# Float64 weights made float32 with the sign and upper exponent on ScalarE and one joining instruction on VectorE, and 34 evictions moved from ScalarE to VectorE

## The chip, the cores and the metric

The kernel runs on one core of one Trainium2 chip. The metric is the device time of one execution in microseconds. Before the change the median of three runs is 370.74 us (370.56 to 374.9). The engines are called PE (TensorE, matrix products), ACT (ScalarE), DVE (VectorE), POOL (GpSimd) and SP (SyncE, which issues the DMA transfers).

## The reference

```python
attn = softmax(mask(q @ k.T / 8)) @ v            # 2 batches x 12 heads, 448 tokens, 64 wide, causal
x = attn as (896 tokens, 768)
x = soft mixture of 8 experts x 4 slots:          # dispatch and combine weights from softmax of x @ phi
    slots = dispatch.T @ x; slot_out = relu(slots @ w1) @ w2; x = combine @ slot_out
out = ((x @ w_a) * (x @ w_b)) @ w_out             # w_a, w_b 768 x 1536, w_out 1536 x 768
```

q, k, v, phi, w1, w2 are float32. The weights w_a, w_b and w_out are drawn and scaled in double precision and come as **float64**: 8 bytes each, 28.3 MB of the 90 MB that the kernel reads. The chip computes in float32, so these 3.5 million numbers have to be turned into float32 inside the kernel.

A float64 has 1 sign bit, 11 exponent bits and 52 mantissa bits. In memory byte 7 (the last) holds the sign and the upper 7 exponent bits, byte 6 the lower 4 exponent bits and the top 4 mantissa bits, and bytes 5, 4 and 3 the next mantissa bits. A float32 of the same number needs the sign, 8 exponent bits with another offset, and the top 23 mantissa bits.

## The kernel before

**Attention stage** (to about 135 us). Heads are taken two at a time, 12 iterations `it`, each in four steps `g` = 0 to 3, in a software pipeline written out by hand (the instruction order of every engine is the order of the code). A step of iteration `it` does: scores of one group of query blocks on PE (`scores`, tile `s`, three PSUM buffers) with the row maxima on DVE (tensor_reduce, tile `nm`); in step 0 also the product with V of iteration it-2 (`pv`, tile `v`, evicted by ACT to `xT`); four transposes of the probabilities of iteration it-1 (`transp`, tile `t` in PSUM, two buffers), whose result is evicted to one quarter of `pT`; the exponentials of the step's scores on ACT (`softmax`, tile `p`); sums and reciprocals on DVE (`norm`, tile `rc`) and the scaling of `p` by them on POOL (line 294). Once per iteration `xtr` turns `xT` back by four transposes (tile `xt`) and evicts them to `x_sb`. The order in which the four quarters of `pT` are turned is `TORD = (1, 3, 0, 2)`. Of them ACT evicts quarters 1, 0 and 2 (line 314); quarter 3 (`TDVE = 1` is its position) is evicted by DVE in `evict`, line 318. ACT also evicts `x_sb`, line 360.

**Conversion.** Between these steps `conv_step` converts one "raw" tile (128 partitions x 768 doubles, 768 KB) at a time; `CVN = (1, 1, 0, 1)` gives three per iteration, after steps 0, 2 and 3. 32 of the 36 raw tiles are converted in the attention stage, the last four (halves of w_out) among the expert products. A raw tile is loaded by SP into one of four ring slots (`NR = 4`), and the slot is free for the next load when DVE has done its part (`used`). Per tile ACT makes two passes (`widen`): line 164 scales the upper word of each double, read as a float32, into the destination, line 165 turns the lower word into an integer in place. One conversion later (`LAG = 1`) DVE joins them in two instructions: line 195 puts the sign bit beside the low bits, line 198 shifts the destination left by three and ORs the low bits in. `widen` and `conv_step` can also put the two passes on POOL, for steps after `LASTQ`; no conversion of the profiled execution does so.

**Expert and output stages** (from about 135 us). The experts' weights w1, w2 stream through the ring (64 tiles of 768 KB), while the combined products of w_a, w_b and w_out are formed beside them.

Of the kernel before, what the change touches and what calls it, by code (L numbers as in the profile page):

```python
# [33 lines left out]
NT1 = 32  # L34
WPRE = (0, 10, 13, 17)
TORD = (1, 3, 0, 2)
SCQ = 1
TDVE = 1
TILES = (
    (("rect", 4, 4, 0, 4), ("rect", 8, 4, 0, 8), ("rect", 12, 4, 0, 12), ("tri", 0, 4), ("sq", 0, 8)),  # L40
    (("rect", 16, 4, 0, 16), ("rect", 20, 4, 0, 13), ("tri", 4, 2)),
# [19 lines left out]
CEND = 1  # L61
# [19 lines left out]
LASTQ = (11, 3)  # L81
# [9 lines left out]
def moe_kernel(ctx: ExitStack, tc: tile.TileContext, pk, vt, phi, w1, w2, wab, wo, rsel, out):  # L91
    nc = tc.nc

    const = ctx.enter_context(tc.tile_pool(name="const", bufs=1))
# [39 lines left out]
    x_sb = {}  # L134
# [11 lines left out]
    raw = {}  # L146

    def load_raw(i, slot):
        t = slot_tile(slot, I32, f"raw{i}")
        nc.sync.dma_start(out=t, in_=(wab[i // 2] if i < 24 else wo[i // 2 - 12])[:, 768 * (i % 2):768 * (i % 2) + 768].bitcast(I32))  # L150
        raw[i] = t

    def widen(t, dst, lo, n, low):
        pr = t.rearrange("p (c w) -> p c w", w=2)[:, lo:lo + n, :]
        hi, lw = pr[:, :, 1].bitcast(F32), pr[:, :, 0].bitcast(U32)
        if low == "pool":
            nc.gpsimd.tensor_scalar(
                out=dst, in0=hi, scalar1=2.0 ** -112, scalar2=1.0, op0=ALU.mult, op1=ALU.mult
            )
            nc.gpsimd.tensor_scalar(  # L160
                out=pr[:, :, 0], in0=lw, scalar1=2.0 ** -29, scalar2=-0.49999, op0=ALU.mult, op1=ALU.add
            )
        else:
            nc.scalar.activation(out=dst, in_=hi, func=AF.Copy, scale=2.0 ** -112)  # L164
            nc.scalar.activation(out=pr[:, :, 0], in_=lw, func=AF.Copy, scale=2.0 ** -29, bias=-0.49999)  # L165
        return dst.bitcast(I32), pr[:, :, 0], pr[:, :, 1]

    conv = []
    fin = []
# [13 lines left out]

    queue_conv(0, 36)

    def conv_step(n, lag=LAG, limit=36, low="act"):
        for _ in range(n):
            if conv and conv[0] < limit:
                i = conv.pop(0)
                dst = conv_dst(i)  # L190
                done.append(i)
                fin.append((i,) + widen(raw[i], dst, 0, 768, low))
            while len(fin) > (lag if conv and conv[0] < limit else 0):
                i, di, b, ph = fin.pop(0)
                nc.vector.scalar_tensor_tensor(  # L195
                    out=b, in0=ph, scalar=-0x80000000, in1=b, op0=ALU.bitwise_and, op1=ALU.bitwise_or
                )
                nc.vector.scalar_tensor_tensor(  # L198
                    out=di, in0=di, scalar=3, in1=b, op0=ALU.logical_shift_left, op1=ALU.bitwise_or
                )  # L200
                used("raw", i)

# [7 lines left out]
    for i in range(2):  # L210
        t = ap.tile([128, PCOLS], F32, name=f"p{i}", bufs=1)
# [87 lines left out]
    def transp(it, b):  # L299
        d = st[it]  # L300
        if b == TORD[0]:
            d["pT"] = ap.tile([128, 16, 128], F32, tag="pT", bufs=1, name=f"pT{it}")
        ps = psT.tile([128, 4, 128], F32, tag="t", name=f"t{it}_{b}")
        for j in range(4):
            kt, i = TBLK[4 * b + j]
            o = POFF[i] + 128 * kt
            nc.tensor.transpose(ps[:, j, :], d["p"][:, o:o + 128], ident)  # L307
        dst = d["pT"][:, 4 * b:4 * b + 4, :]
        if it == 11 and b in (TORD[1], TORD[3]):
            nc.vector.tensor_copy(out=dst, in_=ps)  # L310
        elif it < 11 and b == TORD[TDVE]:
            d["pt"] = dst, ps
        else:
            nc.scalar.activation(out=dst, in_=ps, func=AF.Copy)  # L314

# [189 lines left out]
    with tc.manual_schedule():  # L505
# [15 lines left out]
        for it in range(13):  # L521
            if 1 <= it < 12:
                load_v(it)
            for g in range(4):
                if it == 1:
                    warmup(NW2)
                if it < 12:
                    scores(it, g)
                if g == 0 and it >= 2:
                    pv(it - 2)  # L530
                if it >= 1:
                    transp(it - 1, TORD[g])
                if it < 12:
                    softmax(it, g)
                if g:
                    if it < 12:
                        norm(it, BANKS[g - 1] if it == 11 else ((), BANKS[0] + BANKS[1], BANKS[2])[g - 1])
                elif it:
                    norm(it - 1, BANKS[3])
                if g == SCQ and it + 1 < 12:  # L540
                    begin(it + 1)
                if g == 3 and it + 2 < 12:
                    load_qk(it + 2)
                if (it, g) in DSP:
                    dispatch0(DSP.index((it, g)))
                if it >= 2 and g == (3 if it == 8 else 1):
                    xtr(it - 2)
                if it in (4, 7, 10) and g == 2:
                    logits((it - 4) // 6, (0, 1, 2) if it != 7 else (3, 4, 5))
                step += 1  # L550
                if step > CVOFF:
                    conv_step(CVN[step % len(CVN)], LAG, NT1, "pool" if (it, g) > LASTQ else "act")
                if g == TDVE and 1 <= it < 12:
                    evict(it - 1)
        pv(11)
        xtr(11)
# [688 lines left out]
def layout(inp):  # L1245
    import numpy as np

    q, k, v = inp["q"], inp["k"], inp["v"]
    c = np.ascontiguousarray

    def tr(t):
        return t.reshape(12, 2, S, 64).transpose(0, 1, 3, 2).reshape(12, 128, S)

    v12 = v.reshape(12, 2, S, 64)
    vm = v12[:, :, :384].reshape(12, 2, 3, 128, 64).transpose(0, 3, 2, 1, 4).reshape(12, 128, 384)
    wa, wb, wo = inp["moe2_w_a"], inp["moe2_w_b"], inp["moe2_w_out"]
    rs = np.zeros((64, 5, 2, 128), np.float32)
# [41 lines left out]
```

## Time and profile before

| | |
|---|---|
| median of three runs | 370.74 us |
| span of the profiled execution, first to last instruction | 370.0 us |
| busy in the span: PE, DVE, ACT, POOL | 90%, 62%, 55%, 25% |
| from 20 to 130 us: PE, DVE, ACT, POOL | 99.6, 104.6, 108.2, 71.7 us of 110 |
| mean granted clock of TensorE | 0.985 |

The profiled execution's span is 0.7 us under the median; what lies around the span is not shown. The page's shares are means over stages that differ: in the attention stage ACT and DVE are busy nearly all the time, from 150 to 200 us the DMA queues are, and in the last 70 us PE is. A table by stretches is therefore read before any share of the whole.

### The profile page before, as it was taken

To read this page: it belongs to the slowest core of one execution; us is meant where nothing else is said; L and a number is where in the kernel's file an instruction comes from. 1 tells how busy PE (TensorE), PEld (TensorE's weight loads), DVE (VectorE), ACT (ScalarE), POOL (GpSimd) and SP (SyncE) were. 2 spreads that over 40 slices of the span, in tenths; PEclk is the share of its full clock that TensorE was granted. 3 is DMA by queue.
4 is the path that set the end of the run, shared out by engine and by line. 5 is a ranking of instruction groups with operands and counts; after the bars stand their busy time and mean duration, and the time that the engine had idled before them with its cause. 6 is when DMAs were issued, how large, how long until landed. Compare 5 with 4: busy or idle time off the path is not lost.

```text
span 370.0 us, 6891 instructions
## 1 busy us (share of the span) xinstructions
PE 334.6 (90%) x2551; PEld 201.8 (55%) x2551; DVE 230.1 (62%) x620; ACT 202.0 (55%) x464; POOL 91.1 (25%) x128
## 2 busy tenths in 40 slices
PE   8897898989989978988988889999899889999996
PEld 5454454544544655343342346634565359899995
DVE  3689989999999962021025887507856669933121
ACT  2599999999999952103007445414546732422221
POOL 2457666667766510001000000000000110301110
PEclk9999989999999999999999989999999999999999
DMA  7677789998677787999999999778910000001222
GB/s 282 269 240 282 273 309 389 345 341 288 247 280 280 245 289 308 390 421 416 418 332 402 396 338 351 263 317 272 421 78 2 0 1 2 0 2 43 85 87 85
DMA packets 20224, 90.51 MB, mean 245 GB/s; under 512 B 2336, under 2 KB 5024, under 8 KB 20192
## 3 DMA queue, kind: packets, MB, share of 16 engines
q1 hardware_dynamic: 20192, 90.09, 65.2%
q8 instruction: 20, 0.33, 0.4%
q14 instruction: 12, 0.10, 0.1%
HBM read 87.33 MB, written 2.75 MB: 243 GB/s over the span
## 4 chain that ended last, share of the span: by engine, by line
PE 46%; ACT 27%; DVE 16%; issue 4%; DMA 3%; POOL 3%; ACTq 0%; POOLq 0%; DVEq 0%
ACT p L278 8%; PE o L1172 8%; PE M L891 8%; PE h L651 5%; PE so L692 4%; ACT raw L165 4%; PE ab L777 4%; ACT wab L164 4%; DVE pf L833 3%; ACT pT L314 3%; PE s L257 3%; DVE pt L832 3%; DMA raw<-in_wo_dram 3%; POOL p L294 3%; ACT wo L164 2%
## 5 line engine op out<-in xcount | busy, mean ns | idle before, releaser
L294 POOL TENSOR_SCALAR p<-p,rc 128x448 f32<-128x448 f32 (+6 forms) x84 | 69.2, 837 | 46.4 <-DVE rc L291 36.9
L257 PE MATMUL s<-qk 64*64 64x448 f32 (+6 forms) x336 | 48.5, 403 | 0.1
L1076 POOL TENSOR_TENSOR cc<-gt,cc 128x512 fp32r<-128x512 f32 (+1 forms) x6 | 6.9, 1156 | 157.6 <-ACT cc L1075 157.6
L278 ACT ACTIVATE p<-s,nm 128x448 f32<-128x448 f32 (+6 forms) x84 | 40.0, 492 | 7.8 <-DVE nm L268 7.6
L891 PE MATMUL M<-wt,P_t 128*128 128x384 f32 x168 | 35.9, 356 | 4.1 <-DVE P_t L864 1.3
L307 PE MATMUL t<-ident,p 128*128 128x128 f32 x192 | 33.7, 293 | 5.1 <-POOL p L294 5.1
L195 DVE SCALAR_TENSOR_TENSOR raw<-raw 128x768 int32<-128x768 int32 x36 | 35.2, 978 | 3.0 <-ACT raw L165 3.0
L263 DVE TENSOR_REDUCE nm<-s 128x1 f32<-128x448 f32 (+6 forms) x84 | 31.7, 411 | 8.0 <-PE s L257 8.0
L891 PEld LDWEIGHTS M<-wt,P_t 128*128 128x128 f32 x168 | 29.1, 193 | 13.6 <-ACT wt L885 4.8
L345 PE MATMUL v<-pT,v 128*64 128x448 f32 (+3 forms) x192 | 26.9, 396 | 7.9 <-ACT pT L314 7.7
L165 ACT ACTIVATE raw<-raw 128x768 int32<-128x768 uint32 x36 | 33.9, 941 | 0.0
L651 PE MATMUL h<-w,sT 128*32 128x512 f32 x192 | 29.9, 614 | 3.2 <-DMA w<-in_w_dram 2.3
L257 PEld LDWEIGHTS s<-qk 64*64 64x64 f32 x336 | 19.9, 136 | 21.3 <-issue 15.6
L307 PEld LDWEIGHTS t<-ident,p 128*128 128x128 f32 x192 | 20.7, 142 | 17.6 <-POOL p L294 7.3
L885 ACT ACTIVATE wt<-wo 128x384 fp32r<-128x384 f32 x48 | 21.8, 513 | 13.6 <-PE M L891 13.1
L886 DVE TENSOR_TENSOR wt<-wo,wt 128x384 fp32r<-128x384 f32 x48 | 23.8, 552 | 8.5 <-ACT wt L885 8.5
L198 DVE SCALAR_TENSOR_TENSOR wab<-wab,raw 128x768 int32<-128x768 int32 x24 | 27.9, 1162 | 0.8
L777 PE MATMUL ab<-wab,sT 128*32 128x384 f32 x288 | 27.5, 498 | 0.5 <-DVE sT L616 0.5
L692 PE MATMUL so<-w,hpad 128*32 128x384 f32 x256 | 24.8, 493 | 0.9 <-ACT wt L885 0.4
L314 ACT ACTIVATE pT<-t 128x512 f32<-128x512 f32 x35 | 21.7, 619 | 5.5 <-PE t L307 5.0
L345 PEld LDWEIGHTS v<-pT,v 128*64 128x64 f32 (+1 forms) x192 | 10.9, 134 | 22.6 <-ACT pT L314 14.0
L164 ACT ACTIVATE wab<-raw 128x768 f32<-128x768 f32 x24 | 23.1, 962 | 0.0
(155 smaller groups left out, 519.5 us busy)
## 6 DMA issues: line engine op xcount, KB each, us to landing
w<-in_w_dram SPq DMA_DIRECT2D x64, 768.0 KB, 8.0
raw<-in_wab_dram SPq DMA_DIRECT2D x24, 768.0 KB, 5.3
raw<-in_wo_dram SPq DMA_DIRECT2D x12, 768.0 KB, 4.4
qk<-in_pk_dram SPq DMA_DIRECT2D x12, 448.0 KB, 4.9
v<-in_pk_dram SPq DMA_DIRECT2D x12, 192.0 KB, 5.5
out_dram<-ost SPq DMA_DIRECT2D x6, 384.0 KB, 2.3
v<-in_vt_dram SPq DMA_DIRECT2D x12, 32.0 KB, 5.3
out_dram<-ost SPq DMA_DIRECT2D x2, 192.0 KB, 1.9
```

What stands on the lines that cost most here:

```text
L164: nc.scalar.activation(out=dst, in_=hi, func=AF.Copy, scale=2.0 ** -112)
L165: nc.scalar.activation(out=pr[:, :, 0], in_=lw, func=AF.Copy, scale=2.0 ** -29, bias=-0.49999)
L195: nc.vector.scalar_tensor_tensor(out=b, in0=ph, scalar=-0x80000000, in1=b, op0=ALU.bitwise_and, op1=ALU.bitwise_or)
L257: nc.tensor.matmul(sb[r, o:o + n], lhsT=qT[r, 64 * i:64 * i + 64], rhs=kT[r, 0:n], start=False, stop=True, skip_group_check=True,)
L278: nc.scalar.activation(out=d["p"][:, POFF[i]:POFF[i] + n], in_=sb[:, o:o + n], func=AF.Exp, bias=d["nm"][:, c:c + 1], scale=d["scale"], ac ...
L294: nc.gpsimd.tensor_scalar(out=p[:, POFF[i]:POFF[i] + n], in0=p[:, POFF[i]:POFF[i] + n], scalar1=rc[:, CIX[i]:CIX[i] + 1], scalar2=1.0, op0 ...
L307: nc.tensor.transpose(ps[:, j, :], d["p"][:, o:o + 128], ident)
L345: nc.tensor.matmul(ps[r, 128 * kt:S], lhsT=lhsT, rhs=rhs, start=(kt == 0), stop=(kt == 3), skip_group_check=True)
L651: nc.tensor.matmul(ps[32 * g:32 * g + 32, :], lhsT=sT[:, 0, c, :], rhs=wt[8 * e + i // 3][:, 512 * (i % 3):512 * (i % 3) + 512], start=(i ...
L692: nc.tensor.matmul(so[32 * g:32 * g + 32, 0:384], lhsT=t[:, c, :], rhs=wt[8 * e + 4 + i // 4][:, 384 * (i % 4):384 * (i % 4) + 384], start ...
L777: nc.tensor.matmul(abps[q][32 * g:32 * g + 32, 0:384], lhsT=sT[:, 1, c, :], rhs=w[:, c % 2, 384 * g:384 * g + 384], start=(c == 0), stop=( ...
L891: nc.tensor.matmul(mps[k][h][:, 0:384], lhsT=l[:, f, :], rhs=r, start=(n == 0 and i == 0), stop=(n == 11 and i == 2))
```

## The change

Each raw tile is read from 3 bytes further on, so that a tile's first 32-bit word of each pair holds bytes 3 to 6 of a double, and the byte after it holds byte 7. `wab` and `wo` become flat arrays with 1024 doubles of zeros behind them, so that the last row may run over. The transfer is written in bytes (6144 per partition instead of 1536 words), the bytes that move are as many.

ACT still makes two passes. The first reads byte 7 as a signed 8-bit integer, with the activation function Prelu (one slope for positive and another for negative arguments) and a bias of -56 read from a [128, 1] column `shr`. The second is applied to the first's result in place, again Prelu with a bias column, and writes an integer: the sign and the upper exponent bits in their float32 position. DVE then makes one instruction in place of two: the word of bytes 3 to 6 shifted right by five, ORed into the destination.

Two positions of `TORD` go from ACT to DVE for iterations 0 to 10 (`TDV2 = (2, 3)`, quarters 0 and 2: 22 evictions of 128x512), and all 12 evictions of `x_sb` (112x512). The choice of POOL for late conversions is dropped.

```diff
@@
-TDVE = 1
+TDVE = (1,)
+TDV2 = (2,3)
@@
+    shr = const.tile([128, 2], F32, name="shr")
+    nc.vector.memset(shr[:, 0:1], -56.0)
+    nc.vector.memset(shr[:, 1:2], 112.0 * 2.0 ** -13)
@@ load_raw
-        nc.sync.dma_start(out=t, in_=(wab[i // 2] if i < 24 else wo[i // 2 - 12])[:, 768 * (i % 2):768 * (i % 2) + 768].bitcast(I32))
+        src, n = (wab, i // 2) if i < 24 else (wo, i // 2 - 12)
+        at = (n * 128 * 1536 + 768 * (i % 2)) * 8 + 3
+        rows = src.bitcast(U8)[at:at + 128 * 12288].rearrange("(p b) -> p b", b=12288)
+        nc.sync.dma_start(out=t.bitcast(U8), in_=rows[:, 0:6144])
@@ widen
-            nc.scalar.activation(out=dst, in_=hi, func=AF.Copy, scale=2.0 ** -112)
-            nc.scalar.activation(out=pr[:, :, 0], in_=lw, func=AF.Copy, scale=2.0 ** -29, bias=-0.49999)
+        top = t.bitcast(I8).rearrange("p (c b) -> p c b", b=8)[:, :, 4]
+        nc.scalar.activation(out=dst, in_=top, func=AF.Prelu, bias=shr[:, 0:1], scale=1.0, alpha=2.0 ** -40)
+        nc.scalar.activation(
+            out=dst.bitcast(I32), in_=dst, func=AF.Prelu, bias=shr[:, 1:2], scale=2.0 ** 27, alpha=2.0 ** 40
+        )
@@ conv_step
                 nc.vector.scalar_tensor_tensor(
-                    out=b, in0=ph, scalar=-0x80000000, in1=b, op0=ALU.bitwise_and, op1=ALU.bitwise_or
-                )
-                nc.vector.scalar_tensor_tensor(
-                    out=di, in0=di, scalar=3, in1=b, op0=ALU.logical_shift_left, op1=ALU.bitwise_or
+                    out=di, in0=low, scalar=5, in1=di, op0=ALU.logical_shift_right, op1=ALU.bitwise_or
                 )
@@ transp
-        elif it < 11 and b == TORD[TDVE]:
+        elif it < 11 and TORD.index(b) in TDVE:
             d["pt"] = dst, ps
+        elif it < 11 and TORD.index(b) in TDV2:
+            nc.vector.tensor_copy(out=dst, in_=ps)
@@ xtr
-        nc.scalar.activation(out=x_sb[b][:, :, 128 * pr:128 * pr + 128], in_=ps, func=AF.Copy)
+        nc.vector.tensor_copy(out=x_sb[b][:, :, 128 * pr:128 * pr + 128], in_=ps)
```

What moves is seen best in one iteration of the attention stage (its steps 1 to 3). First ACT, from the exponentials of step 1 (`s_1`) to those of step 3 (`s_3`), before the change; `t_0` and `t_2` are quarters of the transposed probabilities, `xt` the turned attention output, `raw` a raw tile:

```order
L278 ACTIVATE p_129,sm_783<-s_1_887,nm_782 128x384 [waits DVE_49,PE_49,Pool_49]
L278 ACTIVATE p_129,sm_783<-s_1_887,nm_782 128x128 [waits Pool_49]
L360 ACTIVATE x_sb_428<-xt_906 112x4x128 [waits PE_49]
L314 ACTIVATE pT_867<-t_0_921 128x512 [waits PE_49]
L278 ACTIVATE p_129,sm_783<-s_2_913,nm_782 128x320 [waits DVE_49,Pool_49]
L278 ACTIVATE p_129,sm_783<-s_2_913,nm_782 128x192 [waits Pool_49]
L164 ACTIVATE wab_111<-raw_819 128x768 [waits DMAHW6_49]
L165 ACTIVATE raw_819<-raw_819 128x768
L314 ACTIVATE pT_867<-t_2_946 128x512 [waits PE_49]
L278 ACTIVATE p_129,sm_783<-s_3_941,nm_782 128x256 [waits DVE_49,Pool_49]
```

The same place of ACT in the changed kernel:

```order
L277 ACTIVATE p_132,sm_775<-s_1_876,nm_774 128x384 [waits DVE_49,PE_49,Pool_49]
L277 ACTIVATE p_132,sm_775<-s_1_876,nm_774 128x128 [waits Pool_49]
L277 ACTIVATE p_132,sm_775<-s_2_902,nm_774 128x320 [waits DVE_49,PE_49,Pool_49]
L277 ACTIVATE p_132,sm_775<-s_2_902,nm_774 128x192 [waits Pool_49]
L164 ACTIVATE wab_114<-raw_810,shr 128x768 [waits DMAHW6_49]
L165 ACTIVATE wab_114<-wab_114,shr 128x768 [waits Activation_49]
L277 ACTIVATE p_132,sm_775<-s_3_929,nm_774 128x256 [waits DVE_49,Pool_49]
```

Three evictions have left the stretch, and line 165 now waits for ACT's own instruction before it (Activation), which it did not before. Now DVE in the same iteration, from the maxima of step 1, before the change:

```order
L263 TENSOR_REDUCE nm_782<-s_1_887 128x1 [waits PE_49]
L263 TENSOR_REDUCE nm_782<-s_1_887 128x1
L318 COPY pT_867<-t_3_895 128x512 [waits PE_49]
L263 TENSOR_REDUCE nm_782<-s_2_913 128x1 [waits PE_49]
L263 TENSOR_REDUCE nm_782<-s_2_913 128x1
L290 TENSOR_SCALAR rc_784<-sm_783 128x4 [waits Activation_49,Pool_49]
L291 RECIPROCAL rc_784<-rc_784 128x4 [waits DVE_49]
L195 SCALAR_TENSOR_TENSOR raw_765<-raw_765 128x768 [waits DMAHW5_49]
L198 SCALAR_TENSOR_TENSOR wab_111<-wab_111,raw_765 128x768 [waits DVE_49]
L263 TENSOR_REDUCE nm_782<-s_3_941 128x1 [waits PE_49]
```

And in the changed kernel:

```order
L262 TENSOR_REDUCE nm_774<-s_1_876 128x1 [waits PE_49]
L262 TENSOR_REDUCE nm_774<-s_1_876 128x1
L361 COPY x_sb_429<-xt_895 112x4x128 [waits PE_49]
L319 COPY pT_857<-t_3_884 128x512
L262 TENSOR_REDUCE nm_774<-s_2_902 128x1 [waits PE_49]
L262 TENSOR_REDUCE nm_774<-s_2_902 128x1
L313 COPY pT_857<-t_0_910 128x512 [waits PE_49]
L289 TENSOR_SCALAR rc_776<-sm_775 128x4 [waits Activation_49,Pool_49]
L290 RECIPROCAL rc_776<-rc_776 128x4 [waits DVE_49]
L197 SCALAR_TENSOR_TENSOR wab_114<-raw_757,wab_114 128x768 [waits DMAHW5_49]
L262 TENSOR_REDUCE nm_774<-s_3_929 128x1 [waits PE_49]
L313 COPY pT_857<-t_2_934 128x512 [waits PE_49]
```

DVE has one joining instruction where it had two, and three more copies out of PSUM, each of which waits for PE in DVE's order.

## Rows read from the trace of the kernel before

**Rows 1.** Busy time by stretch; columns: PE, PEld, DVE, ACT, POOL busy, clock, DMA, GB/s.

```profile
40.00:50.00 10.00, 8.53 (x55) 4.36 (x51) 8.75 (x16) 9.87 (x24) 6.59 (x8) 0.83 0.82 302
...
20.00:130.00 110.00, 99.56 (x761) 53.16 (x759) 104.62 (x209) 108.22 (x257) 71.67 (x83) 0.98 0.84 297
150.00:200.00 50.00, 44.88 (x436) 19.15 (x428) 8.76 (x19) 9.90 (x15) 1.90 (x9) 1.00 1.02 399
```

**Rows 2.** Chain that ended last, from 67 to 80 us, by engine and line.

```profile
by line: ACT p L278 34.0%; ACT wab L164 25.0%; ACT raw L165 19.4%; issue 12.2%; ACT pT L314 10.3%; ACT xT L349 6.7%; ACT x_sb L360 1.1%; ACTq L314 0.1%
```

**Rows 3.** ACT in order of time, one iteration; columns: start, duration, instruction, idle before.

```profile
68.19 0.63 ACT L278 ACTIVATE p<-s,nm 128x448 f32<-128x448 f32 x1
...
69.09 0.93 ACT L164 ACTIVATE wab<-raw 128x768 f32<-128x768 f32 x1
69.91 0.90 ACT L165 ACTIVATE raw<-raw 128x768 int32<-128x768 uint32 x1
70.69 0.59 ACT L278 ACTIVATE p<-s,nm 128x384 f32<-128x384 f32 x1
...
71.58 0.61 ACT L360 ACTIVATE x_sb<-xt 112x512 f32<-112x512 f32 x1
72.06 0.62 ACT L314 ACTIVATE pT<-t 128x512 f32<-128x512 f32 x1
72.54 0.56 ACT L278 ACTIVATE p<-s,nm 128x320 f32<-128x320 f32 x1
...
78.72 0.63 ACT L278 ACTIVATE p<-s,nm 128x448 f32<-128x448 f32 x1
```

**Rows 4.** ACT groups from 20 to 130 us, shapes apart; count, busy us, mean ns.

```profile
L349 ACT ACTIVATE xT<-v 128x448 f32<-128x448 f32 x10 | 5.7, 574 | 0.0
...
L278 ACT ACTIVATE p<-s,nm 128x448 f32<-128x448 f32 x10 | 6.4, 641 | 0.0
```

**Rows 5.** DVE in order of time, the same iteration.

```profile
70.47 0.68 DVE L318 COPY pT<-t 128x512 f32<-128x512 f32 x1
71.07 0.74 DVE L263 TENSOR_REDUCE nm<-s 128x1 f32<-128x320 f32 x2
...
72.11 0.93 DVE L195 SCALAR_TENSOR_TENSOR raw<-raw 128x768 int32<-128x768 int32 x1
73.08 1.27 DVE L198 SCALAR_TENSOR_TENSOR wab<-wab,raw 128x768 int32<-128x768 int32 x1
```

**Rows 6.** DVE in order of time, a late conversion while POOL is idle.

```profile
192.99 0.96 DVE L195 SCALAR_TENSOR_TENSOR raw<-raw 128x768 int32<-128x768 int32 x1
193.99 0.96 DVE L198 SCALAR_TENSOR_TENSOR wo<-wo,raw 128x768 int32<-128x768 int32 x1
```

**Rows 7.** POOL in order of time, same iteration: six passes, and one of them.

```profile
72.39 5.35 POOL L294 TENSOR_SCALAR p<-p,rc 128x448 f32<-128x448 f32 x6 [1.06 <-DVE rc L291]
...
73.53 1.01 POOL L294 TENSOR_SCALAR p<-p,rc 128x64 f32<-128x64 f32 x1
```

**Rows 8.** POOL groups from 20 to 130 us by shape, two that wait least.

```profile
L294 POOL TENSOR_SCALAR p<-p,rc 128x384 f32<-128x384 f32 x11 | 7.7, 702 | 0.6 <-ACT x_sb L360 0.6
L294 POOL TENSOR_SCALAR p<-p,rc 128x128 f32<-128x128 f32 x11 | 4.7, 430 | 0.0
```

**Rows 9.** PE in order of time, the same iteration: its two waits.

```profile
75.74 1.34 PE L345 MATMUL v<-pT,v 128*64 128x320 f32 x12 [1.22 <-ACT pT L314]
...
77.80 0.33 PE L307 MATMUL t<-ident,p 128*128 128x128 f32 x1 [0.24 <-POOL p L294]
```

**Rows 10.** All engines in order of time, end of the attention stage.

```profile
131.97 0.96 DVE L195 SCALAR_TENSOR_TENSOR raw<-raw 128x768 int32<-128x768 int32 x1 [0.36 <-ACT raw L165]
...
132.97 0.96 DVE L198 SCALAR_TENSOR_TENSOR wo<-wo,raw 128x768 int32<-128x768 int32 x1
...
134.35 0.48 POOL L294 TENSOR_SCALAR p<-p,rc 128x256 f32<-128x256 f32 x1 [3.54 <-DVE rc L291]
```

**Rows 11.** DMA issues of the whole execution: count, KB each, us to landing.

```profile
raw<-in_wab_dram SPq DMA_DIRECT2D x24, 768.0 KB, 5.3
```

More of the change, by code (lines that the diff above doesn't have):

```diff
@@ L14 @@
 U32 = mybir.dt.uint32
+I8 = mybir.dt.int8
+U8 = mybir.dt.uint8
 AF = mybir.ActivationFunctionType
@@ L50 @@
 LAG = 1
-CVN = (1, 1, 0, 1)
+CVN = (1,1,0,1)
 STAGES = (3, 5)
@@ L149, in load_raw, with widen @@
         t = slot_tile(slot, I32, f"raw{i}")
-        nc.sync.dma_start(out=t, in_=(wab[i // 2] if i < 24 else wo[i // 2 - 12])[:, 768 * (i % 2):768 * (i % 2) + 768].bitcast(I32))
+        src, n = (wab, i // 2) if i < 24 else (wo, i // 2 - 12)
+        at = (n * 128 * 1536 + 768 * (i % 2)) * 8 + 3
+        rows = src.bitcast(U8)[at:at + 128 * 12288].rearrange("(p b) -> p b", b=12288)
+        nc.sync.dma_start(out=t.bitcast(U8), in_=rows[:, 0:6144])
         raw[i] = t
[L153 to L158, printed above, removed]
-            )
[L160 to L163, printed above, removed]
-            nc.scalar.activation(out=dst, in_=hi, func=AF.Copy, scale=2.0 ** -112)
-            nc.scalar.activation(out=pr[:, :, 0], in_=lw, func=AF.Copy, scale=2.0 ** -29, bias=-0.49999)
-        return dst.bitcast(I32), pr[:, :, 0], pr[:, :, 1]
+    def widen(t, dst):
+        top = t.bitcast(I8).rearrange("p (c b) -> p c b", b=8)[:, :, 4]
[3 more added lines that the diff above has]
+        )
+        return dst.bitcast(U32), t.bitcast(U32).rearrange("p (c w) -> p c w", w=2)[:, :, 0]
     conv = []
@@ L184, in moe_kernel, with conv_step @@
     queue_conv(0, 36)
-    def conv_step(n, lag=LAG, limit=36, low="act"):
+    def conv_step(n, lag=LAG, limit=36):
         for _ in range(n):
@@ L191, in conv_step @@
                 done.append(i)
-                fin.append((i,) + widen(raw[i], dst, 0, 768, low))
+                fin.append((i,) + widen(raw[i], dst))
             while len(fin) > (lag if conv and conv[0] < limit else 0):
-                i, di, b, ph = fin.pop(0)
+                i, di, low = fin.pop(0)
                 nc.vector.scalar_tensor_tensor(
-                    out=b, in0=ph, scalar=-0x80000000, in1=b, op0=ALU.bitwise_and, op1=ALU.bitwise_or
-                )
-                nc.vector.scalar_tensor_tensor(
-                    out=di, in0=di, scalar=3, in1=b, op0=ALU.logical_shift_left, op1=ALU.bitwise_or
+                    out=di, in0=low, scalar=5, in1=di, op0=ALU.logical_shift_right, op1=ALU.bitwise_or
                 )
@@ L551, in moe_kernel @@
                 if step > CVOFF:
-                    conv_step(CVN[step % len(CVN)], LAG, NT1, "pool" if (it, g) > LASTQ else "act")
-                if g == TDVE and 1 <= it < 12:
+                    conv_step(CVN[step % len(CVN)], LAG, NT1)
+                if g in TDVE and 1 <= it < 12:
                     evict(it - 1)
@@ L557, in moe_kernel @@
         logits(1, (3, 4, 5))
-        conv_step(CEND, LAG, NT1, "pool")
+        conv_step(CEND, LAG, NT1)
         att.close()
@@ L622, in moe_kernel @@
         xctx.close()
-        conv_step(99, LAG, NT1, "pool")
+        conv_step(99, LAG, NT1)
         r3 = ctx.enter_context(tc.tile_pool(name="r3", bufs=1, side="right", reuse_waits="tile"))
@@ L1256, in layout @@
     wa, wb, wo = inp["moe2_w_a"], inp["moe2_w_b"], inp["moe2_w_out"]
+    end = np.zeros(1024, wo.dtype)
     rs = np.zeros((64, 5, 2, 128), np.float32)
@@ L1268, in layout @@
         "w2": c(inp["moe_w2"].reshape(8, 2, 4, 128, 768).transpose(0, 1, 3, 2, 4).reshape(8, 2, 128, 3072)),
-        "wab": c(np.concatenate([wa.reshape(6, 128, 1536), wb.reshape(6, 128, 1536)])).view(np.int64),
-        "wo": c(wo.reshape(6, 2, 128, 768).transpose(0, 2, 1, 3).reshape(6, 128, 1536)).view(np.int64),
+        "wab": c(np.concatenate([wa.reshape(-1), wb.reshape(-1), end])).view(np.int64),
+        "wo": c(np.concatenate([wo.reshape(6, 2, 128, 768).transpose(0, 2, 1, 3).reshape(-1), end])).view(np.int64),
         "rsel": rs.reshape(64, 1280),
```

## The prediction

> **What bounds the kernel now.** I read the busy times by stretch first, since the page's shares are means over stages with different limits. From 20 to 130 us ACT is busy 108.2 of 110 us and DVE 104.6, PE 99.6, and the DMA share is 0.84; from 150 to 200 us ACT and DVE do next to nothing and the DMA share is 1.02 [rows 1]. The change acts on ACT and DVE, so it is worth something in the first stretch. Two engines look full there; the chain of waits says which of them counts: from 67 to 80 us it stays on ACT but for "issue" [rows 2]. The reader is to see that no DVE, PE or POOL line stands in it.
>
> Then I read one undisturbed iteration of ACT. It runs from the exponential at 68.19 to the next at 78.72, 10.53 us, without a gap: an instruction starts when the one before it is nearly through [rows 3]. What an instruction costs ACT is therefore the distance between starts, not its duration: an eviction costs 0.48 us (71.58 to 72.06, 72.06 to 72.54) though it takes 0.61 to 0.62, and a conversion's two passes cost 1.60 (69.09 to 70.69) though they take 0.93 and 0.90.
>
> A second loop has the same length, and it has to be cleared before ACT's relief can count. The first exponential of an iteration, a conversion and the second pair of exponentials pass before POOL can start its six scalings at 72.39; these take 5.35 us, to 77.74 [rows 7]; the last transpose that waits for them runs from 77.80 to 78.13 [rows 9]; its eviction and then the next exponential, at 78.72, close the loop. PE's other wait is 1.22 us for an eviction that ACT makes late [rows 9].
>
> **The change part by part.**
>
> *Evictions off ACT.* 22 of `pT` and, before the last iteration's, 11 of `x_sb` leave ACT: 33 x 0.48 = 15.8 us. They go to DVE, where such a copy costs 0.60 (70.47 to 71.07) [rows 5].
>
> *ACT's two passes.* The trace has no Prelu, no 8-bit input and no pass of ACT that waits for the one before it. I go through three things. (a) A bias read from a column: the exponential has one and takes 641 ns at 128x448, the plain copy of that size 574 [rows 4]: 0.07 more each, twice. (b) The second pass reads what the first wrote, so the overlap goes: it starts at the first's end, not 0.11 before it (69.09 + 0.93 = 70.02, against 69.91) [rows 3]; DVE's own dependent pair shows a gap of 0.04 after the end (192.99 + 0.96 = 193.95, next at 193.99) [rows 6]. Together 0.15. (c) The second pass becomes contiguous and the first reads single bytes, as many elements and 8 bytes apart as before; no row shows either, and I count nothing. Sum 2 x 0.07 + 0.15 = 0.29 per conversion. Ends: 0.14 (only the bias) and 0.48 (the break-even below), since the write of the first pass has to be seen by the second and ACT's own wait may be longer than DVE's. 32 conversions x 0.29 = 9.3 us.
>
> The Trainium skill, "ScalarE: Activation LUTs", section "What ACT_TABLE_LOAD costs", speaks against this part more strongly: each column operand adds about 93 ns, where the rows give 67. By that estimate the conversions cost 0.05 more each, 1.7 us in all.
>
> *ACT's iteration.* 10.53 - 3 x 0.48 + 3 x 0.29 = 9.96 us. Over the stage: 15.8 - 9.3 = 6.5 us less.
>
> *DVE.* Per iteration three first instructions go (each costs 0.97, 72.11 to 73.08 [rows 5]), three copies of 0.60 come: 1.1 us less. The join that stays has the operands of line 198, one contiguous and one strided input. It takes 1.27 beside POOL and 0.96 without [rows 5, 6]; I take 1.0. So DVE does not become the limit by its sum, 10.53 - 1.1 = 9.4. But its copies stand in order behind PE: `x_sb` waits for four transposes that PE makes after `t_3`, and the maxima of step 2 are queued behind both copies; the exponentials of step 2 wait for these maxima. ACT now comes to them earlier by the two evictions that stood there. The cover is DVE's 1.1 us of slack. If it is not enough, ACT waits some tenths per iteration.
>
> *POOL's loop.* Line 294 on 64 elements took 1.01 us while line 198 ran, on 128 elements 0.43 in the mean, on 384 0.70 [rows 7, 8]: POOL waits while DVE works on two SBUF tensors. The two means give 0.36 to 0.77 us for 64 to 448 elements, 3.4 us for the six passes, so some 2.0 of the 5.35 are waits. Half of DVE's two-tensor instructions go, so I take 1.0 off. The loop becomes 10.53 + 0.29 - 1.0 = 9.8, just under ACT's 9.96. PE's wait of 1.22 goes too: the late quarter is now copied by DVE right behind the maxima of step 3. PE's own work is 10.53 - 1.22 - 0.24 = 9.1.
>
> *The end of the stage.* The last conversion's ACT passes, DVE pair, reciprocal and POOL scaling follow one another (131.97, 132.97, 134.35) [rows 10]. One DVE instruction of 1.0 goes there, 0.29 on ACT comes: 0.7 us less.
>
> *The rest.* The four late conversions: ACT 0.29 longer, DVE 1.0 shorter each, and other products need both engines there; I take 0.2 us more. The columns `shr` are set on DVE while it waits for POOL's identity: nothing. From 150 us the DMA queues are full [rows 1], but their stream starts when the last raw tiles leave the ring, so it moves forward with the stage's end and gives nothing back.
>
> *The transfers.* As many bytes and rows of 6144, from an address 3 bytes off. No row shows such a read. Below, nothing. Above: three raw tiles of 768 KB among 3,000 KB per iteration (by the shapes) are 77% of the bytes; at 0.84 share and 10.53 us [rows 1, 3], an iteration of 9.96 us needs 0.89 of the queues, and they are full when the raw rows take 1.16 times as long. The raw tile lands 5.3 us after its issue [rows 11], with four slots of about 3.3 us each. I take nothing, since the nearest rows, the same transfers, leave that margin.
>
> The Trainium skill, "DMA: Bandwidth & Descriptors", section "How a descriptor splits into AXI transactions", states that only the first transaction of a misaligned descriptor begins below its start; as an estimate that is one 32-byte beat more on 192 per row. No run here shows it; by that the transfers cost nothing either.
>
> *Sum.* 6.5 + 0.7 - 0.2 = 7.0 us. The iteration around 45 us does not follow ACT (the granted clock is 0.83 of 2.4 GHz from 40 to 50 us, so PE ran partly at the lower level [rows 1]), and ACT will meet some of DVE's new waits: I take 1.0 off. 370.0 - 6.0 = 364.0 for the profiled execution; the median of the runs is 0.7 above its span, so **364.7**.
>
> **The rivals.**
> 1. *All of ACT's relief, and the others follow* (the dependent pair costs no more than today's 1.60). ACT's iteration is then 10.53 - 1.44 = 9.1, as PE's, and the POOL loop has to lose 1.4 too. For it: both PE waits go. Against: (a) has a row. 10 x 1.44 + 0.5, less 3 for the iterations that carry other work: 12, so 359.
> 2. *POOL's loop holds.* The scalings wait as long as before, since the passes begin right behind a join and the new copies delay the reciprocals. The loop is then 10.53 + 0.29, and ACT waits at its eviction of `t_1`. It decides where POOL saves less than 0.29 us of its six passes. Price: 10 x 0.29 - 0.7 + 0.2 = +2.4: 373. For it: the loop is exactly as long as ACT's today. Against it: the 64-element row.
> 3. *The change does nothing for ACT*: a pair costs 0.48 more (a slow 8-bit read, a longer own wait), and 3 x 0.48 pays back the evictions. Only the end's 0.5 is left: 370.
> 4. *The misaligned rows are slow.* At 1.5 times as long, the queues are full at 0.84 x 10.53 x (0.77 x 1.5 + 0.23) = 12.3 us per iteration, 1.8 more than today: 10 x 1.8 = 18 us, 388. It is slower than before from 1.25 times. For it: no row shows such a read; against: margin up to 1.16.
>
> **Chances.** Forecast 0.50 (361 to 368, from the ends of the pair's cost: 32 x 0.15 less to 32 x 0.1 more), rival 1 0.18, rival 2 0.10, rival 3 0.12, rival 4 0.10. The range 359 to 372 leaves out rival 4, most of rival 2 and the far side of rival 1. What a measurement of this kernel can tell from no change is about 2%, 7.4 us, here 363.3: rival 1 and two fifths of the forecast lie below it, 0.38; over 2% slower are rival 4 and a remnant, 0.10; within, 0.52.
>
> **What would show it.** In the profile after: exponentials of 128x448 some 10.0 us apart; ACT without gaps; line 165 starting just after line 164 ends, and the next instruction 1.9 us after the pair's start; the six passes of POOL in 4.4 us; PE without the wait for `pT`; raw transfers landing in 5 to 6 us. The prediction is wrong if ACT shows waits for PE `t` (rival 2) or for DVE `nm` of step 2, if the pair costs 2.1, or if ACT's line 164 waits for DMA (rival 4).

## The result, and the profile after

The changed kernel takes 360.72 us (median of four runs, 358.98 to 364.55), against 370.65 for the kernel before in the same comparison: 0.973 of it, with a 95% interval of 0.969 to 0.977. That is 9.9 us less, where 6.0 were forecast. The time lies in the range of 359 to 372; the gain exceeds 2%, the case to which 0.38 was given. The profiled execution has a span of 356.9 us, 13.1 less than before; some of these 13.1 us are not the change's, see below.

The page of the changed kernel, busy time by engine and the chain that ended last:

```profile
PE 329.5 (92%) x2551; PEld 200.6 (56%) x2551; DVE 212.4 (59%) x620; ACT 192.2 (54%) x430; POOL 73.0 (20%) x128
...
PE 56%; DVE 21%; ACT 10%; POOL 6%; DMA 3%; issue 3%; POOLq 0%; DVEq 0%; ACTq 0%
```

The chain of the kernel before:

```profile
PE 46%; ACT 27%; DVE 16%; issue 4%; DMA 3%; POOL 3%; ACTq 0%; POOLq 0%; DVEq 0%
```

PE is now most of the chain, and ACT's share fell from 27% to 10%. Busy time by stretch, with the columns of [rows 1]:

```profile
20.00:120.00 100.00, 96.11 (x755) 52.20 (x753) 90.10 (x207) 98.59 (x227) 53.13 (x83) 1.00 0.89 326
...
140.00:190.00 50.00, 45.09 (x424) 19.31 (x420) 6.84 (x17) 10.76 (x15) 1.91 (x9) 0.97 1.02 399
```

In the attention stage ACT is as full as before, DVE fell from 0.95 to 0.90 of the stretch and POOL from 0.65 to 0.53. PE rose from 0.91 to 0.96, because the same work is done in less time. Now ACT in order of time, one iteration, from one long exponential (128x448, one per iteration) to the next; this answers to [rows 3]:

```profile
62.54 0.64 ACT L277 ACTIVATE p<-s,nm 128x448 f32<-128x448 f32 x1
...
63.44 1.00 ACT L164 ACTIVATE wab<-raw,shr 128x768 f32<-128x768 int8 x1
64.47 0.94 ACT L165 ACTIVATE wab<-wab,shr 128x768 int32<-128x768 f32 x1
65.32 0.56 ACT L277 ACTIVATE p<-s,nm 128x384 f32<-128x384 f32 x1
...
71.32 0.53 ACT L350 ACTIVATE xT<-v 128x448 f32<-128x448 f32 x1
71.74 0.59 ACT L315 ACTIVATE pT<-t 128x512 f32<-128x512 f32 x1
72.22 0.64 ACT L277 ACTIVATE p<-s,nm 128x448 f32<-128x448 f32 x1
```

The iteration lasts 72.22 - 62.54 = 9.68 us, against 10.53 before and 9.96 forecast. A conversion's pair costs 65.32 - 63.44 = 1.88 (forecast 1.89), and line 165 starts 0.03 after line 164 ends (64.44). ACT's column of idle time is empty. In the kernel before, the same two evictions at the end of the iteration stood thus (ACT in order of time):

```profile
77.59 0.58 ACT L349 ACTIVATE xT<-v 128x448 f32<-128x448 f32 x1
78.23 0.60 ACT L314 ACTIVATE pT<-t 128x512 f32<-128x512 f32 x1
```

Their starts were 0.64 apart, now 0.42. The 0.22 is ACT's wait for the transpose `t_1`, which ends at 78.13 because POOL's scalings end late [rows 7, 9]. It is no accident of this iteration: over the ten iterations from 20 to 130 us of the kernel before the distance goes from 0.42 to 0.90, 0.64 in the mean; in the changed kernel it is 0.42 or 0.43 but for once (0.81). POOL and PE in the changed kernel, in order of time:

```profile
67.00 3.97 POOL L293 TENSOR_SCALAR p<-p,rc 128x448 f32<-128x448 f32 x6 [0.98 <-ACT p L277]
```

```profile
68.64 1.34 PE L346 MATMUL v<-pT,v 128*64 128x320 f32 x12
70.62 0.73 PE L306 MATMUL t<-ident,p 128*128 128x128 f32 x4 [0.64 <-POOL p L293]
```

The six scalings take 3.97 us, against 5.35 before and 4.4 forecast. PE waits no longer for `pT`; the wait for POOL, 0.24 before, is 0.64. The end of the stage, all engines, answers to [rows 10]:

```profile
121.85 0.96 DVE L197 SCALAR_TENSOR_TENSOR wo<-raw,wo 128x768 uint32<-128x768 uint32 x1 [1.18 <-ACT wo L165]
...
123.24 0.48 POOL L293 TENSOR_SCALAR p<-p,rc 128x256 f32<-128x256 f32 x1 [2.27 <-DVE rc L290]
```

**Where the 13.1 us of the two profiles lie.** The first long exponential starts at 7.51 where it started at 8.46. No changed conversion or eviction has run by then, and the experiments' profiles scatter over the same stretch (7.35 to 8.46), so this 0.95 is not put down to the change. From the third (24.69, now 23.73) to the twelfth (122.39, now 112.89) 97.70 became 89.16: 8.5 us less, of which 1.2 belong to the iteration around 45 us, slowed before by a spell at a lower clock [rows 1] that the changed kernel's profile does not show there. About 1.6 comes between the twelfth exponential and the first expert output; the parts between there and 291 us gain 0.35 together. The last 79.4 us became 77.8; no instruction there differs, but before had a spell of 3.4 us at the lower clock there (294.2 to 297.6, granted clock 0.51, the 1.2 GHz level; PE had been busy 8.92 of the 10 us before it). So 0.95 us of the start and 1.2 + 1.6 of the clock, 3.8 in all, are not the change's, and some 9.3 are, near the medians' 9.9. The runs say the same in another way. In every run whose span is known the time is 2.0 to 2.2 us above the span, so the profiled execution before, with 370.0, took about 372.1, some 1.4 above its median; the one after, with 358.98, lies 1.7 below its own.

### The profile page after: what moved, and what is told of

Read it like the earlier page. It is cut to its first block, busy times and chain, and to the rows that moved or that the text cites. A ratio compares the mean times of both kernels' runs of the same rounds, so it can differ in the third digit from the quotient of the medians.

```text
span 356.9 us, 6864 instructions
## 1 busy us (share of the span) xinstructions
PE 329.5 (92%) x2551; PEld 200.6 (56%) x2551; DVE 212.4 (59%) x620; ACT 192.2 (54%) x430; POOL 73.0 (20%) x128
## 4 chain that ended last, share of the span: by engine, by line
PE 56%; DVE 21%; ACT 10%; POOL 6%; DMA 3%; issue 3%; POOLq 0%; DVEq 0%; ACTq 0%
PE o L1173 8%; PE M L892 7%; PE s L256 7%; POOL p L293 6%; PE t L306 5%; PE h L652 5%; PE so L693 5%; PE ab L778 4%; DVE pf L834 4%; DMA raw<-in_wo_dram 3%; DVE pt L833 3%; ACT p L277 2%; PE v L346 2%; DVE pf L845 2%; PE hp L672 2%
## 5 line engine op out<-in xcount | busy, mean ns | idle before, releaser
L293 POOL TENSOR_SCALAR p<-p,rc 128x448 f32<-128x448 f32 (+6 forms) x84 | 54.1, 658 | 40.7 <-DVE rc L290 21.0
L256 PE MATMUL s<-qk 64*64 64x448 f32 (+6 forms) x336 | 46.7, 391 | 1.1 <-DMA qk<-in_pk_dram 1.1
L277 ACT ACTIVATE p<-s,nm 128x448 f32<-128x448 f32 (+6 forms) x84 | 38.6, 468 | 7.3 <-DVE nm L267 7.1
L306 PE MATMUL t<-ident,p 128*128 128x128 f32 x192 | 32.1, 289 | 4.2 <-POOL p L293 4.2
L197 DVE SCALAR_TENSOR_TENSOR wab<-raw,wab 128x768 uint32<-128x768 uint32 x24 | 24.1, 1003 | 3.7 <-ACT wab L165 3.7
L164 ACT ACTIVATE wab<-raw,shr 128x768 f32<-128x768 int8 x24 | 24.3, 1011 | 0.0
L165 ACT ACTIVATE wab<-wab,shr 128x768 int32<-128x768 f32 x24 | 22.5, 936 | 0.8
L834 DVE TENSOR_TENSOR pf<-abt 128x12 f32<-128x12 f32 (+19 forms) x95 | 21.7, 243 | 0.0
L1073 DVE TENSOR_TENSOR gt<-gt,c 128x512 f32<-128x512 f32 (+2 forms) x12 | 6.5, 542 | 23.3 <-ACT gt L1072 23.3
L164 ACT ACTIVATE wo<-raw,shr 128x768 f32<-128x768 int8 x12 | 12.2, 1018 | 15.0 <-DMA raw<-in_wo_dram 15.0
```

Of the source, the lines that this page charges most:

```text
L164: nc.scalar.activation(out=dst, in_=top, func=AF.Prelu, bias=shr[:, 0:1], scale=1.0, alpha=2.0 ** -40)
L256: nc.tensor.matmul(sb[r, o:o + n], lhsT=qT[r, 64 * i:64 * i + 64], rhs=kT[r, 0:n], start=False, stop=True, skip_group_check=True,)
L277: nc.scalar.activation(out=d["p"][:, POFF[i]:POFF[i] + n], in_=sb[:, o:o + n], func=AF.Exp, bias=d["nm"][:, c:c + 1], scale=d["scale"], ac ...
L293: nc.gpsimd.tensor_scalar(out=p[:, POFF[i]:POFF[i] + n], in0=p[:, POFF[i]:POFF[i] + n], scalar1=rc[:, CIX[i]:CIX[i] + 1], scalar2=1.0, op0 ...
L834: nc.vector.tensor_tensor(out=view(p), in0=ops[0][0], in1=ops[0][1], op=ALU.mult)
```

## The experiments

Two theories stood against each other. A: ACT's sum of starts sets the iteration, the conversion's extra cost is paid for by the evictions, and the joins that DVE loses make room for them. B: the new conversion is itself the gain (fewer instructions on DVE, less blocking of POOL), and the evictions only change sides.

**The conversion alone.** The evictions go back to ACT:

```diff
-TDV2 = (2,3)
+TDV2 = ()
@@ xtr
-        nc.vector.tensor_copy(out=x_sb[b][:, :, 128 * pr:128 * pr + 128], in_=ps)
+        nc.scalar.activation(out=x_sb[b][:, :, 128 * pr:128 * pr + 128], in_=ps, func=AF.Copy)
```

> The new conversion alone: all evictions stay where they were before the change. Theory A (the attention stage runs at the sum of ACT's distances between starts): 9.69 us of the changed kernel plus the three evictions that come back, 3 x 0.48, gives 11.13 us per iteration against 10.53 before the change, so about 10 x 0.6 - 0.5 = 5.5 us slower than before the change, some 376 us. Rival B (the gain comes from DVE's 36 fewer instructions and the POOL scalings that wait for them): as fast as the changed kernel or nearly, 361 to 364 us. By both the six POOL scalings take about 4.0 us instead of 5.35, since DVE has one two-tensor instruction per conversion.

Measured: 377.65 us against 369.86, 1.020 times (1.015 to 1.024). The long exponentials are 11.11 apart (11.13 expected). Busy by stretch, then POOL in order of time:

```profile
20.00:120.00 100.00, 86.49 (x649) 45.98 (x647) 62.21 (x156) 98.63 (x223) 39.59 (x72) 0.98 0.84 296
```

```profile
53.01 3.26 POOL L293 TENSOR_SCALAR p<-p,rc 128x448 f32<-128x448 f32 x6 [3.84 <-DVE rc L290]
```

DVE falls to 62% and POOL's six scalings to 3.26 us, and the kernel is slower, since ACT is full and longer. B falls: what DVE and POOL save does not pay for what ACT gains in work while ACT is the limit. One thing it does buy. All evictions are on ACT here, as before the change, and yet the two at the end of an iteration start 0.42 apart in eight of the nine iterations. The iteration is 10.53 + 3 x 0.28 - 11.11 = 0.26 us shorter than the old one with dearer pairs: with POOL's scalings shorter, ACT's wait for `t_1` is gone.

**The evictions alone.** The old conversion and the old transfers, with the evictions on DVE. Cut from the difference to the changed kernel:

```diff
-        nc.scalar.activation(out=dst, in_=top, func=AF.Prelu, bias=shr[:, 0:1], scale=1.0, alpha=2.0 ** -40)
...
+            nc.scalar.activation(out=dst, in_=hi, func=AF.Copy, scale=2.0 ** -112)
+            nc.scalar.activation(out=pr[:, :, 0], in_=lw, func=AF.Copy, scale=2.0 ** -29, bias=-0.49999)
@@ conv_step
-                    out=di, in0=low, scalar=5, in1=di, op0=ALU.logical_shift_right, op1=ALU.bitwise_or
+                    out=b, in0=ph, scalar=-0x80000000, in1=b, op0=ALU.bitwise_and, op1=ALU.bitwise_or
+                )
+                nc.vector.scalar_tensor_tensor(
+                    out=di, in0=di, scalar=3, in1=b, op0=ALU.logical_shift_left, op1=ALU.bitwise_or
```

> The old conversion with the evictions moved to DVE. Theory A: ACT's iteration would be 10.53 - 1.44 = 9.1 us or less, so ACT no longer sets it; DVE's sum does, 10.53 + 3 x 0.60 = 12.3 us per iteration, some 18 us slower than before the change, about 388 us, with DVE busy without gaps. Rival B': the evictions are what counts and DVE takes them in its gaps: faster than before the change, near 362 us. The six POOL scalings take 5.3 us or more.

Measured: 387.99 us, 1.048 times (1.043 to 1.053). Busy by stretch, and the chain from 63 to 75 us by line:

```profile
20.00:120.00 100.00, 85.67 (x597) 44.65 (x595) 94.81 (x192) 77.18 (x185) 58.46 (x65) 0.93 0.78 269
```

```profile
by line: DVE raw L196 31.4%; DVE wab L199 29.7%; DVE nm L264 17.0%; DVE pT L315 10.0%; DVE pT L321 5.0%; DVE x_sb L363 5.0%; issue 4.3%; DVE rc L291 2.9%; DVE rc L292 2.1%
```

The chain is all DVE but for "issue", and ACT has 23% to spare: the exponentials are 12.04 us apart (75.15 to 87.19). Each half alone makes the kernel slower, by 7.8 and 18.1 us; together they make it 9.9 faster. Theory A needs just that: the evictions take the load off the engine that the conversion burdens, and the conversion off the engine that the evictions burden.

**Is the lost overlap to be had back?** The exponentials of a step go between the two passes, so that line 165 (167 here) no longer waits for line 164:

```diff
+    half = []
+    def conv_first(n, limit=36):
+        if n and conv and conv[0] < limit:
...
+            widen_a(raw[i], dst)
+            half.append((i, dst))
@@ step of an iteration, after the transposes
+                if step + 1 > CVOFF:
+                    conv_first(CVN[(step + 1) % len(CVN)], NT1)
                 if it < 12:
                     softmax(it, g)
```

> The changed kernel with the step's exponentials between the two ACT passes of a conversion, so that the second pass no longer stands right behind the first that it reads. Theory A: the lost overlap, 0.15 us per conversion, comes back: ACT's iteration 9.69 - 0.45 = 9.24 us, 4 us faster than the changed kernel, about 356.5 us; PE's own 9.1 us per iteration is then nearly the limit. Rival C (DVE and PE are already as late as ACT in the changed kernel): no change, 360 to 361 us, with gaps on ACT.

Measured: 361.41 us, 0.975 (0.968 to 0.981), as the changed kernel. ACT in order of time, then DVE, then PE:

```profile
54.06 1.02 ACT L164 ACTIVATE wab<-raw,shr 128x768 f32<-128x768 int8 x1
54.95 0.65 ACT L289 ACTIVATE p<-s,nm 128x448 f32<-128x448 f32 x1
...
55.85 0.96 ACT L167 ACTIVATE wab<-wab,shr 128x768 int32<-128x768 f32 x1
56.67 0.60 ACT L289 ACTIVATE p<-s,nm 128x384 f32<-128x384 f32 x1
...
62.39 0.58 ACT L362 ACTIVATE xT<-v 128x448 f32<-128x448 f32 x1
63.06 0.60 ACT L327 ACTIVATE pT<-t 128x512 f32<-128x512 f32 x1
```

```profile
54.64 0.75 DVE L274 TENSOR_REDUCE nm<-s 128x1 f32<-128x384 f32 x2 [0.61 <-PE s L268]
```

```profile
62.29 0.73 PE L318 MATMUL t<-ident,p 128*128 128x128 f32 x4 [0.62 <-POOL p L305]
```

The overlap returns (the passes' steps are 0.89 and 0.82, 1.71 together), but the long exponentials come 9.43 to 9.63 apart where the iteration carries no other work, not the 9.24 expected: another loop holds ACT, and its two evictions at the end start 0.67 apart again.

**What do the columns cost, and which loop is next?** Both passes as plain copies with a constant bias. This leaves the weights' signs out.

```diff
-func=AF.Prelu, bias=shr[:, 0:1], scale=1.0, alpha=2.0 ** -40)
+func=AF.Copy, bias=-56.0, scale=1.0)
@@
-func=AF.Prelu, bias=shr[:, 1:2], scale=2.0 ** 27, alpha=2.0 ** 40
+func=AF.Copy, bias=0.01, scale=2.0 ** 27
```

> The changed kernel with plain copies with constant bias in place of the two Prelu passes; signs are lost, so its numbers are not the reference's. It prices the bias columns. By the rows of the trace (0.07 us each) a pair costs 1.74 instead of 1.88 us and ACT's iteration is 9.27, 4 us less than the changed kernel; by 0.093 us each a pair costs 1.69 and the iteration 9.13 us, 5 us less, if PE allows it. Rival: the columns cost nothing and the pair stays at 1.88.

Measured: 359.96 us, 0.969 (0.962 to 0.977), not to be told from the changed kernel. ACT in order of time, one pair; ACT's groups from 20 to 120 us (count, busy us, mean ns) of this kernel, then of the changed one:

```profile
55.10 0.91 ACT L164 ACTIVATE wab<-raw 128x768 f32<-128x768 int8 x1
56.04 0.84 ACT L165 ACTIVATE wab<-wab 128x768 int32<-128x768 f32 x1
56.79 0.56 ACT L277 ACTIVATE p<-s,nm 128x384 f32<-128x384 f32 x1
```

```profile
L164 ACT ACTIVATE wab<-raw 128x768 f32<-128x768 int8 x24 | 22.2, 924 | 0.0
L165 ACT ACTIVATE wab<-wab 128x768 int32<-128x768 f32 x24 | 20.2, 843 | 0.8
```

```profile
L164 ACT ACTIVATE wab<-raw,shr 128x768 f32<-128x768 int8 x23 | 23.3, 1012 | 0.0
L165 ACT ACTIVATE wab<-wab,shr 128x768 int32<-128x768 f32 x24 | 22.5, 936 | 0.8
```

The pair costs 1.69 instead of 1.88; the passes are 88 and 93 ns shorter. The Trainium skill, "ScalarE: Activation LUTs", section "What ACT_TABLE_LOAD costs", says about 93 ns for a column operand; this run agrees with it, and not with the 67 that I took from [rows 4]. The edit takes away Prelu together with the column; no run here prices the two apart. Three pairs give 0.57 per iteration, yet the exponentials are 9.49 us apart (63.70 to 73.19), only 0.2 closer. The chain of waits from 54 to 63.6 us, its pieces in order of time (start, us, what), shows why:

```profile
54.74 0.59 PE t L306 x4
55.32 0.45 PE xt L358 x4
...
55.80 0.69 DVE x_sb L361
56.49 0.60 DVE pT L319
57.09 0.66 DVE nm L262 x2
...
58.46 0.19 DVE rc L290
...
58.83 2.28 POOL p L293 x4
61.10 0.12 issue
61.22 1.17 POOL p L293
62.39 0.05 issue
62.44 0.73 PE t L306 x4
```

The next limit, a loop, lies 0.2 us under ACT: transposes, DVE's copies and reciprocals, POOL's six scalings, and again PE's transposes.

**Can that loop be shortened by order alone?** DVE copies `t_3` before `x_sb`, and makes the reciprocals before the copy of `t_0`:

```diff
@@ transp
+        elif it < 11 and TORD.index(b) == 2:
+            d["pu"] = dst, ps
@@ step of an iteration, after norm
+                if g == 2 and 1 <= it < 12:
+                    dst, ps = st[it - 1].pop("pu")
+                    nc.vector.tensor_copy(out=dst, in_=ps)
...
@@ after evict
+                if g == 1:
+                    x_evict()
```

> The changed kernel with two places swapped in DVE's order: quarter 3 of pT is copied before x_sb, and the reciprocals of the first four columns come before the copy of quarter 0. In the two runs that relieved ACT further, an iteration stayed at 9.5 us, set by a loop over DVE's maxima and copies, the reciprocals, POOL's six scalings, the transposes and the next scores. Theory A: ACT's 9.69 us is still the longest in the changed kernel, so this alone changes nothing: 360 to 361 us. Rival C: the loop over DVE and POOL already sets the changed kernel: about 0.4 us less per iteration, 357 us.

Measured: 362.22 us, 0.976 (0.971 to 0.980); the long exponentials are 9.79 to 9.87 apart, no closer than the changed kernel's 9.68 to 9.73. With ACT as the limit the order on DVE is worth nothing. Then both edits together, the split passes and the order:

> Both edits: the exponentials between the two ACT passes, and the swapped order on DVE. Theory A with the loop as the next limit: ACT's sum 9.24 us, the loop 9.5 - 0.3 (reciprocals earlier) - 0.26 (no wait for xt) = 8.95 us, PE 9.1 us: 9.25 us per iteration, 0.44 less than the changed kernel, about 356.5 us. Rival: the loop doesn't shorten and the iteration stays at 9.5, 359 to 361 us.

Measured: 361.11 us, 0.975 (0.971 to 0.980), the exponentials 9.64 to 9.83 apart. My expectation of 9.25 was wrong. ACT in order of time shows the new wait:

```profile
61.27 0.59 ACT L364 ACTIVATE xT<-v 128x448 f32<-128x448 f32 x1
62.16 0.60 ACT L329 ACTIVATE pT<-t 128x512 f32<-128x512 f32 x1 [0.30 <-PE t L318]
62.66 0.99 ACT L164 ACTIVATE wab<-raw,shr 128x768 f32<-128x768 int8 x1
63.56 0.61 ACT L289 ACTIVATE p<-s,nm 128x448 f32<-128x448 f32 x1
```

The loop of PE and POOL closes through ACT's eviction of `t_1`, and the first pass, put ahead of the long exponential, lengthens it by 0.9 us. So that eviction goes to DVE too:

```diff
-TDVE = (1,)
+TDVE = (0, 1)
```

> As split_order, and the last quarter of pT that ACT evicts goes to DVE too (copied at the end of step 0). ACT's sum is then 8.8 us and PE's own work, 9.1 us, is the limit: 9.15 us per iteration, 0.1 less than split_order, 355.5 to 356.5 us. Rival: DVE's copy stands before the maxima of step 1 and lengthens the loop by up to 0.6 us: 9.5 us and 360 us.

Measured: 359.54 us, 0.963 (0.958 to 0.968); the 355.5 to 356.5 expected did not come. It is faster than the kernel before, and probably than the changed one: its interval lies below the changed kernel's and below those of the three others run beside it (0.971 at the lowest), and from the third long exponential to the twelfth 87.5 us pass, against 89.2. But its six runs go from 355.67 to 361.35 and overlap with the changed kernel's, and its iterations are uneven (8.70 to 10.53 us where they carry no other work). Busy by stretch, and ACT's waits from 20 to 120 us (total us, times, longest):

```profile
20.00:120.00 100.00, 97.06 (x773) 53.22 (x768) 94.88 (x223) 92.97 (x218) 59.34 (x83) 1.00 0.91 333
```

```profile
ACT xT L364 <- PE v L360: 4.6, 6, 1.5
ACT wab L164 <- DMA raw<-in_wab_dram: 1.7, 1, 1.7
```

ACT has 7% to spare and waits for PE, which is busy 97% of the stretch. The changed kernel's PE was at 96%, so these edits had little left to gain.

**Does the 3-byte offset cost anything?** Each row is read from its own start, as it was. The weights come out as next to nothing, since the bytes of the exponent are then elsewhere.

```diff
-        at = (n * 128 * 1536 + 768 * (i % 2)) * 8 + 3
+        at = (n * 128 * 1536 + 768 * (i % 2)) * 8
@@ widen
-func=AF.Prelu, bias=shr[:, 0:1], scale=1.0,
+func=AF.Prelu, bias=shr[:, 0:1], scale=2.0 ** -20,
@@ conv_step
-                    out=di, in0=low, scalar=5,
+                    out=di, in0=low, scalar=9,
```

> The changed kernel with the raw rows read from their own start instead of 3 bytes further on. The bytes then mean something else: the first pass multiplies the byte it reads by 2^-20 and the join shifts by nine, so that all weights of the last product come out as next to nothing; every instruction keeps its form and size. Theory A: the 3 bytes cost nothing: 360 to 361 us, and the same DMA share for the same GB/s. Rival D: misaligned rows are slower: raw transfers land sooner than 6.4 us and the time falls by 2 us or more.

Measured: 361.97 us, 0.975 (0.971 to 0.979), as the changed kernel. DMA issues of the page (count, KB, us to landing) of this kernel and of the changed one:

```profile
raw<-in_wab_dram SPq DMA_DIRECT2D x24, 768.0 KB, 6.2
```

```profile
raw<-in_wab_dram SPq DMA_DIRECT2D x24, 768.0 KB, 6.4
```

A raw tile lands 0.2 us earlier, in four slots that have that to spare. That it landed in 5.3 before [rows 11] is therefore not the offset's doing: the conversion alone reads with the offset too, and its page has 5.3. In the changed kernel as much data moves in less time (DMA share 0.89, before 0.84). The estimate that I made from the Trainium skill, "DMA: Bandwidth & Descriptors", section "How a descriptor splits into AXI transactions", one beat more per row, is not contradicted.

## Why the prediction was right, and where its size was off

- The time lies in the range, but not where the forecast put itself: 360.72 is just under the "361 to 368" of its chance of 0.50, and nearer to rival 1's 359 than to 364.7. The lower end is itself added wrongly, 364.7 - 32 x 0.15 = 359.9.
- *What bounds the kernel* was right: ACT, by the sum of its starts. The two single-part runs show it, as does ACT's idle column (0.5 us of waits in the changed kernel from 20 to 120 us).
- *Evictions off ACT*, 0.48 each, were right: with the three back on ACT (the conversion alone) the iteration is 11.11 - 9.68 = 1.43 longer. *The pair*, 0.29 more, came out at 0.28, and that is in part luck, since two errors cancelled inside it. The columns, with Prelu, cost 0.19 instead of 0.14. The broken overlap and the contiguous second pass cost 0.09 instead of 0.15: without columns the steps are 0.94 and 0.75, against 0.82 and 0.78 in [rows 3].
- *ACT's iteration* is the term that was mis-sized: 9.96 forecast, 9.68 measured. I subtracted three evictions from the 10.53 as if ACT had waited for nothing in it, because the rows show no gap. They hid 0.22 us, ACT's wait for `t_1`, and the distance of 0.64 between the starts of two evictions showed it. When POOL became faster that wait went, as the conversion alone shows too (0.26): 10.53 - 1.44 + 3 x 0.28 - 0.22 = 9.71. That is a quarter of a microsecond in ten iterations, 2 to 3 us.
- *The 1.0 taken off* for DVE's new waits and the iteration around 45 us did not come. ACT waits for no maxima, and the profile after has no lower clock there (43.11 to 52.84, 9.73 us); the second is chance, not the change. The two items, 2 to 3 and 1.0, make up most of the 3.9 us by which the gain exceeded the forecast.
- *DVE*: 1.1 less per iteration forecast, 10.53 x 0.951 - 9.68 x 0.901 = 1.3 measured. Rival 1 asked for a pair at today's price, which did not come; 9.9 of its 12 us came all the same, in part by another road, the wait that POOL's shorter scalings took off ACT.
- *POOL's loop* (rival 2) fell: the six scalings lost 1.38 us, not under 0.29. The reason given stands, and can be counted: of DVE's instructions on two SBUF tensors, four ran beside the six scalings before (from 72.11, 73.08, 75.23 and 76.28), two do in the changed kernel (66.72 and 69.15), one in the conversion alone (52.74), and the scalings take 5.35, 3.97 and 3.26 us: some 0.7 us for each. One pass shows it by itself: on 128x320 it takes 1.16 us in the changed kernel (69.40), beside the instruction of 69.15, and 0.52 in the conversion alone (55.35), beside none. The price in the prediction was too low: by 0.7 for each some 2.6 us are left without any, not 3.4, and 2.8 of the 5.35 were waits, not 2.0. The Trainium skill, "SBUF — State Buffer", section "Who interferes with whom", says that a DVE instruction with two SBUF inputs contends with a GpSimd one that reads SBUF; these three agree.
- *The end of the stage*: from the last join's start to the start of POOL's last scaling 2.38 before (131.97 to 134.35), 1.39 now (121.85 to 123.24); 1.0 less, and 0.28 more on ACT, so 0.7 as forecast.
- *The 0.7 between span and median* is the distance of two executions and not what lies around a span, which is 2.0 to 2.2 in every run; as it was added to before and after alike, the forecast gain of 6.0 is untouched.
- *The transfers* cost nothing (rival 4 fell), and *rival 3* fell with the pair's 1.88.

That the changed kernel's runs see fewer spells at the lower clock is not shown: the experiments' profiles have them at other places and in other number, and what starts one stays open.

## What to carry to other kernels

Trading work between two full engines can pay although each half of the trade loses; price both engines with all moves applied, and run the halves to see that the gain is in the pair. A row of starts without gaps can still hide a wait: compare the distance between starts with that of the same two instructions where nothing is awaited. Before relieving the limiting engine further, take the busy share of the others in the same stretch; here PE at 96% left under 4 us in 100.

## What the runs showed of the hardware that I had not expected

- A pass of ACT that reads what the pass before it wrote starts 0.03 us after that one's end; when exponentials stand between them, the passes advance by 0.89 and 0.82. Chaining two passes costs 1.88 - 1.71 = 0.17 us, not a long wait.
- Each DVE instruction on two SBUF tensors that runs beside POOL's scalings costs them 0.6 to 0.7 us, a little under what is left of it when the pass starts: before, 0.65, 0.82, 0.76 and 0.83 us of it were left at 72.39, 73.53, 75.48 and 76.62, and these four passes took 1.16, 1.01, 1.16 and 1.12.
- An 8-bit input 8 bytes apart costs no more than a 32-bit one: 924 ns in the mean with a constant bias, against 962 for line 164 before, from 20 to 130 us.
- Rows of 6144 bytes read from an address 3 bytes off take no measurable time more.
